# Attention into a cosine-gated FFN on one core: float64 weights turned into float32 in two engine passes instead of three, with the stored bytes shifted by two and a new hand order

## The chip, the cores and the metric

The kernel runs on one core of one Trainium2 chip. The metric is the device time of one execution in microseconds (us), the median of several runs. The kernel before takes 707.85 us (three runs, 706.53 to 709.95).

## What is computed

Eight batches, eight heads, 576 tokens, head size 64, 32 memory slots, then a feed-forward layer over all 4608 tokens:

```python
a = softmax(phi, axis=seq)                      # (b, h, s, m)
k_m = einsum('bhsm,bhsd->bhmd', a, k); v_m = einsum('bhsm,bhsd->bhmd', a, v)
attn = softmax(q @ k_m.T / sqrt(64)) @ v_m      # (b, h, s, d)
x = attn.transpose(0, 2, 1, 3).reshape(4608, 512)
h = x @ w_in                                    # w_in: 512 x 2048
out = (h * cos(h)) @ w_out                      # w_out: 2048 x 512
```

The inputs are float32, but `w_in` and `w_out` are float64: the drawn numbers are scaled without a cast. [...]

## The kernel before, in words

**Tiling.** The 4608 tokens are worked in 12 groups of 384, so that two batches of 576 make three groups. The hidden dimension of 2048 is cut into 16 slices f of 128. For each group and each f there is a first product (`gemm1`, tile `hp`), a chain on ScalarE (ACT) and VectorE (DVE) for h·cos(h) (tiles `gp` and `u`), and a second product (`gemm2`, tile `acc`) that adds up over f, four slices behind the first. `v_m` is folded into `w_in` beforehand (`fold_first` for group 0, tile `pvf`, kept as `vf`; `fold_psum` for the rest, tiles `pv` and `vw`), so that `gemm1` multiplies softmax weights (`aT`) by folded weights. Group 0 works in float32 on the converted weights as they are; from group 1 on every operand is split into a float16 high and low part, once the largest weight is known.

**Weights.** Each weight matrix comes in eight blocks, in0 to in7 and out0 to out7, 1024 KB of float64 each, 8 KB on each of 128 partitions. Blocks in2 and in3 are parked in the part of `wo` that later holds out6, out7 and out4, out5; the other fourteen take turns in three buffers, raw0 to raw2, and a load waits until its buffer's last block has been converted. Block in(j) is needed by fold_first(j), which serves gemm1 of slices 2j and 2j+1 of group 0; block out(j) by gemm2 of the same slices.

**Conversion before** (`conversion`, lines 156 to 185). Of each 8-byte word: *low* (L171 on ACT, L166 on DVE or POOL) writes the low 16 bits of the result from a byte of the lower word; *scale* (L175 on ACT, L176 on POOL) multiplies the upper word, read as float32, by 2^-112 in place, which moves the exponent; *sign* (L179, DVE) writes the upper 16 bits with the sign; *join* (L181, DVE) shifts the scaled word left by three and ORs it in. A *square* (L184, ACT) then sums the squares for the largest weight. That is four conversion instructions and a square for each of 16 blocks, each over 128x1024 elements.

**Order.** Group 0, the attention of batch 0 and the start of batch 1, the conversions and all their loads stand in one order written out by hand: the string `ORDER`, whose names are steps. Each engine runs its own steps in that order, and SyncE's (SP's) queue issues the loads in it. `warm*n` is n matmuls on zeros that keep TensorE (PE) busy and compute nothing; all 75 of them stand ahead of the first `gemm1`. From group 1 on a scheduler lays out the instructions.

The steps at the start, in the order of their dependence: load `phiT` and turn it into softmax weights (`max0`, `e0`, PE transposes `w0`, copies `k0`, L745); gather over tokens with the five loaded parts of k and v (`ga0_0` to `ga0_4`, L258, tile `psA`); normalise (`X0`, L780 and L782), transpose (`tpx0`, L787), spread into `km` (L270, L271) and `vm`; scores (`sc0`, L403) with the loaded `q`; on DVE transpose (`tu0`, L409), maximum (`mx0`, L413), subtract (`sh0`, L420), on ACT exp (`ex0`, L416), on DVE sum (`to0`, L424 to L426), normalise (`no0`, L430), transpose back (`ba0`, L434, into `aT`); and with the folded block in0 the first `gemm1` (`g1_0`, L561).

Of the kernel before, what the change touches and what calls it, by code (L numbers as in the profile page):

```python
# [23 lines left out]
P = 128  # L24
# [9 lines left out]
NW = DF // WS  # L34
GT = 384
# [8 lines left out]
LOW_ACT = set('in0 in2 in6 in7 out2 out3 out6 out7'.split())  # L44
LOW_POOL = set('in3 in4 out1 out4 out5'.split())
SCALE_ACT = set('in1 in2 in3 in4 in6 in7 out0 out5'.split())
COPY_ACT = set('vm1'.split())
# [27 lines left out]
def attention_then_ffn(ctx: ExitStack, tc: tile.TileContext, phi, phiT, kv, kv_first, qT, w_in, w_out, eye, out):  # L75
# [18 lines left out]
    w_in_sb = const.tile([P, NP, DF], F32, name="w_in_sb")  # L94
# [61 lines left out]
    def conversion(dst, raw, sq_to):  # L156

        high = raw[:, :, :, 1]  # L160
        flat = raw.rearrange("p c f t -> p c (f t)")
        halves = dst.bitcast(I16).rearrange("p c (f t) -> p c f t", t=2)
        low_top = flat.bitcast(U8).rearrange("p c (f t) -> p c f t", t=8)[:, :, :, 3]
        high_top = flat.bitcast(I8).rearrange("p c (f t) -> p c f t", t=8)[:, :, :, 7]
        def low_bits(engine):
            engine.tensor_scalar(out=halves[:, :, :, 0], in0=low_top, scalar1=2.0 ** -5, scalar2=-31.0 / 64.0,  # L166
                                 op0=ALU.mult, op1=ALU.add)

        spare = junk.rearrange("p (c f) -> p c f", c=dst.shape[1])
        return {  # L170
            "low_ACT": lambda: nc.scalar.activation(halves[:, :, :, 0], low_top, AF.Copy, scale=2.0 ** -5,  # L171
                                                    bias=-31.0 / 64.0),
            "low_DVE": lambda: low_bits(nc.vector),
            "low_POOL": lambda: low_bits(nc.gpsimd),
            "scale_ACT": lambda: nc.scalar.mul(high.bitcast(F32), high.bitcast(F32), 2.0 ** -112),  # L175
            "scale_POOL": lambda: nc.gpsimd.tensor_scalar(out=high.bitcast(F32), in0=high.bitcast(F32),  # L176
                                                          scalar1=2.0 ** -112, scalar2=1.0, op0=ALU.mult,
                                                          op1=ALU.mult),
            "sign": lambda: nc.vector.tensor_scalar(out=halves[:, :, :, 1], in0=high_top, scalar1=0.0,  # L179
                                                    scalar2=-32768.0, op0=ALU.is_lt, op1=ALU.mult),  # L180
            "join": lambda: nc.vector.scalar_tensor_tensor(out=dst.bitcast(I32), in0=high, scalar=3,  # L181
                                                           in1=dst.bitcast(I32), op0=ALU.logical_shift_left,
                                                           op1=ALU.bitwise_or),
            "square": lambda: nc.scalar.activation(spare, dst, AF.Square, accum_out=sq_to),  # L184
        }

    def convert(kind, j):
        if kind == "in":
            return conversion(w_in_sb[:, :, j * WS:(j + 1) * WS], loads.pop(("in", j)), sq[:, 0, j:j + 1])
        return conversion(wo[:, 2 * j + 1:2 * j + 3], loads.pop(("out", j)), sq[:, 1, j:j + 1])  # L190
# [32 lines left out]
    def w_in_split(q, c):  # L223
        if c == 0:
            st["parts"] = ld.tile([P, 2, NP, FS], F16, tag=f"raw{1 + q % 2}", name=f"w_in_parts_{q}")
        parts, s, src = st["parts"], st["s", "in"], w_in_sb[:, c, q * FS:(q + 1) * FS]
        nc.scalar.activation(parts[:, 0, c], src, AF.Copy, scale=s)
        nc.vector.scalar_tensor_tensor(out=parts[:, 1, c], in0=src, scalar=s, in1=parts[:, 0, c],
                                       op0=ALU.mult, op1=ALU.subtract)
        if c < NP - 1:  # L230
            return
        if q == 0:
            w2 = ld.tile([P, NP, 2, FS], F16, tag="raw0", name="w_in_2_0")
        else:
            w2 = w_in_sb[:, :, (q - 1) * FS:q * FS].bitcast(F16).rearrange("p c (o f) -> p c o f", o=2)
# [285 lines left out]
    def fold_first(j):  # L521
        pv = small_ps(f"pvf_{j}").rearrange("p (g x) -> p g x", g=2)
        for g in range(2):
            for i in range(2):
                c = 2 * g + i
                nc.tensor.matmul(pv[D * i:D * (i + 1), g], lhsT=st["vm", 0][:, c],  # L526
                                 rhs=w_in_sb[:, c, j * WS:(j + 1) * WS], start=True, stop=True)
# [331 lines left out]
    junk = wk.tile([P, 4 * WS], BF16, tag="aT", name="junk", bufs=3)  # L859
    for kind, j in blocks:  # L860
# [3 lines left out]
        def step(what, kind=kind, j=j, make=make):  # L864
            if not make:
                make.update(convert(kind, j))
            make[what]()
        low = "ACT" if name in LOW_ACT else "POOL" if name in LOW_POOL else "DVE"
        put(f"low_{name}", lambda step=step, low=low: step("low_" + low))
# [232 lines left out]
```

## Time and profile before

| What | Value |
|---|---|
| Median of three runs | 707.85 us (706.53 to 709.95) |
| The profiled execution's own time | 707.53 us |
| Its span (first to last instruction) | 705.4 us |
| PE busy | 695.0 us, 99% |
| DVE busy | 536.0 us, 76% |
| ACT busy | 515.6 us, 73% |
| POOL busy | 31.2 us, 4% |
| Moved by DMA | 66.17 MB |

Busy time is counted from the start of an instruction to its modelled end; PE's matmuls are pipelined, so a busy PE is not always a PE at its peak. The chain of waits is the work that ended last, followed back from the end: at each step to what released it. A row such as `L181 DVE ... x8 | 10.2, 1281 | 0.1` is a group of eight instructions of line 181, 10.2 us busy together, 1281 ns each, with 0.1 us of idle time of the engine before them. Where rows give a start, it is in us from the start of the span.

### The profile page before, as it was taken

The numbers are of one execution on the slowest core, as the hardware profiler recorded it, in microseconds if no ns is written. First come the engines' busy times: TensorE is split into PE (matmuls) and PEld (weight loads), VectorE is DVE, ScalarE is ACT, GpSimd is POOL, SyncE is SP. The second block draws the span as 40 slices with busy tenths as digits, with TensorE's granted clock in tenths as the row PEclk, the third lists the DMA queues.
The fourth block names the chain that finished last, engine by engine and source line by source line (L and its number), as shares of the span: only waits on it lengthen the run. The fifth ranks groups of instructions, "written<-read, shape, count | busy, mean of one in ns | idle before, by whom it ended". The sixth has DMA issues, their size and how long they took to land.

```text
span 705.4 us, 11869 instructions
## 1 busy us (share of the span) xinstructions
PE 695.0 (99%) x4607; PEld 355.9 (50%) x4607; DVE 536.0 (76%) x1130; ACT 515.6 (73%) x953; POOL 31.2 (4%) x43
## 2 busy tenths in 40 slices
PE   8999999999999999999999999999999999999997
PEld 3444455554444445655444445655444445565553
DVE  3899999999988876589667896579766986566552
ACT  3699897998985976869766885769757775665652
POOL 1122300000001000010000000000000000000000
PEclk9999999999999999999999999999999999999999
DMA  9998815128344200332105300152100100100101
GB/s 288 388 346 313 303 51 149 34 61 239 103 98 135 110 1 1 110 105 68 46 1 169 113 0 2 46 170 68 46 0 2 41 5 2 46 1 1 46 1 45
DMA packets 31480, 66.17 MB, mean 94 GB/s; under 512 B 2176, under 2 KB 11456, under 8 KB 31424
## 3 DMA queue, kind: packets, MB, share of 16 engines
q1 hardware_dynamic: 27104, 57.55, 25.4%
q10 hardware_dynamic: 4320, 7.87, 3.0%
q8 instruction: 36, 0.59, 0.4%
q14 instruction: 20, 0.16, 0.1%
HBM read 51.77 MB, written 9.44 MB: 87 GB/s over the span
## 4 chain that ended last, share of the span: by engine, by line
PE 82%; DVE 7%; ACT 7%; DMA 3%; issue 1%; SPq 0%; DVEq 0%; ACTq 0%
PE acc L621 40%; PE hp L570 22%; PE acc L616 6%; PE pv L500 4%; PE hp L561 3%; PE psA L258 3%; PE sc L403 2%; DMA phi<-in_phi 2%; DVE u L591 1%; PE warm L659 1%; ACT gp L586 1%; DMA raw_in<-in_w_in 1%; ACT u L596 1%; DVE u L600 1%; PE pv L494 1%; PE pvf L526 1%
## 5 line engine op out<-in xcount | busy, mean ns | idle before, releaser
L621 PE MATMUL acc<-wo,gp 128*128 128x512 f16 x1584 | 371.9, 379 | 0.0
L621 PEld LDWEIGHTS <-gp 128*128 128x128 f16 x1584 | 153.5, 98 | 159.3 <-issue 1.0
L570 PE MATMUL hp<-aT,vw 128*128 128x192 f16 (+1 forms) x1440 | 203.5, 284 | 1.6 <-DVE u L600 1.5
L570 PEld LDWEIGHTS <-vw 128*128 128x128 f16 x1440 | 124.9, 98 | 83.9 <-issue 29.1
L596 ACT ACTIVATE u<-u,quarter 128x384 f32<-128x384 f32 x176 | 106.7, 614 | 70.9 <-DVE u L591 70.4
L600 DVE SCALAR_TENSOR_TENSOR u<-hp,u 128x384 f32<-128x384 f32 x176 | 96.3, 553 | 60.8 <-ACT u L596 60.1
L591 DVE SCALAR_TENSOR_TENSOR u<-hp,cu,gp 128x192 f32<-128x192 f32 (+1 forms) x240 | 115.3, 503 | 23.7 <-ACT gp L586 22.1
L586 ACT ACTIVATE gp<-hp,cu 128x192 int32<-128x192 f32 (+1 forms) x240 | 110.9, 491 | 20.4 <-PE hp L570 15.2
L603 DVE TENSOR_TENSOR gp<-u,gp 128x384 f16<-128x384 f32 x176 | 96.1, 552 | 35.2 <-ACT gp L602 35.0
L602 ACT CAST gp<-u 128x384 f16<-128x384 f32 x176 | 88.0, 508 | 41.1 <-DVE u L600 40.4
L616 PE MATMUL acc<-wo,gp 128*128 128x512 f32 x96 | 44.4, 599 | 0.0
L509 DVE SCALAR_TENSOR_TENSOR vw<-pv,vw 128x512 f16<-128x512 f32 x48 | 33.0, 687 | 7.1 <-ACT vw L507 6.6
L507 ACT ACTIVATE vw<-pv 128x512 f16<-128x512 f32 x48 | 28.4, 591 | 8.7 <-PE pv L500 8.2
L637 ACT ACTIVATE ob<-acc,os 128x512 f32<-128x512 f32 x28 | 18.5, 684 | 14.8 <-PE acc L621 12.1
L616 PEld LDWEIGHTS acc<-wo,gp 128*128 128x128 f32 x96 | 17.5, 190 | 19.6 <-issue 16.3
L258 PE MATMUL psA<-kv,phi 128*32 128x129 f32 (+3 forms) x640 | 24.0, 277 | 1.1 <-ACT w_in_sb L171 0.6
L561 PE MATMUL hp<-aT,vf 128*128 128x384 f32 x64 | 23.9, 499 | 0.1
L596 ACT ACT_TABLE_LOAD x18 | 23.1, 1283 | 0.3
L258 PEld LDWEIGHTS psA<-kv,phi 128*32 128x32 f32 (+1 forms) x640 | 16.0, 109 | 13.8 <-issue 7.8
L659 PE MATMUL warm<-zeros 128*128 128x512 f16 x75 | 19.6, 402 | 1.8 <-DVE zeros L654 1.8
L403 PE MATMUL sc<-q,km 128*64 128x256 f32 (+3 forms) x192 | 20.0, 336 | 0.8 <-issue 0.8
L416 ACT ACT_TABLE_LOAD x14 | 18.0, 1283 | 0.2
(164 smaller groups left out, 550.8 us busy)
## 6 DMA issues: line engine op xcount, KB each, us to landing
kv<-in_kv SPq DMA_DIRECT2D x28, 516.0 KB, 6.4
raw_out<-in_w_out SPq DMA_DIRECT2D x8, 1024.0 KB, 7.2
q<-in_qT SPq DMA_DIRECT2D x7, 1152.0 KB, 5.6
out<-ob ACTq DMA_DIRECT2D x30, 256.0 KB, 2.1
raw_in<-in_w_in SPq DMA_DIRECT2D x6, 1024.0 KB, 9.8
phi<-in_phi SPq DMA_DIRECT2D x7, 512.0 KB, 6.1
w_in_sb<-w_in_parts SPq DMA_DIRECT2D x12, 256.0 KB, 5.6
phiT<-in_phiT SPq DMA_DIRECT2D x4, 576.0 KB, 7.8
```

The lines of the kernel that those rows point to most:

```text
L258: nc.tensor.matmul(psA[32 * j:32 * (j + 1), g * KV:g * KV + wide], lhsT=a[:n, c, h * M:(h + 1) * M], rhs=kvs[c][:n, h * wide:(h + 1) * wid ...
L403: nc.tensor.matmul(sc[D * p:D * (p + 1), g * n:(g + 1) * n], lhsT=km[:, 2 * g + p], rhs=qt[:, 2 * g + p, t0:t0 + n], start=True, stop=True)
L561: nc.tensor.matmul(hp[:, :GT], lhsT=st["vf", q][:, g, fo * P:(fo + 1) * P], rhs=st["aTf"][:, g], start=(g == 0), stop=(g == 1))
L570: nc.tensor.matmul(hp[:, c0:c0 + n], lhsT=vw[:, wi, g, fo * P:(fo + 1) * P], rhs=aT[:, ai, g, c1:c1 + n], start=(k == 0), stop=(k == 5))
L586: ins = nc.scalar.activation(ni[:, c0:c0 + n], hp[:, c0:c0 + n], AF.Copy, scale=turns, bias=0.25)
L591: nc.vector.scalar_tensor_tensor(out=u[:, c0:c0 + n], in0=hp[:, c0:c0 + n], scalar=turns, in1=ni[:, c0:c0 + n], op0=ALU.mult, op1=ALU.subt ...
L596: nc.scalar.activation(u, u, AF.Sin, scale=TWO_PI_BELOW, bias=quarter)
L600: nc.vector.scalar_tensor_tensor(out=u, in0=hp[:, :GT], scalar=2.0 ** -17, in1=u, op0=ALU.mult, op1=ALU.mult)
L602: nc.scalar.copy(gp[:, 0], u)
L603: nc.vector.tensor_tensor(out=gp[:, 1], in0=u, in1=gp[:, 0], op=ALU.subtract)
L616: nc.tensor.matmul(accs[grp][t], lhsT=gp[:, t * P:(t + 1) * P], rhs=wo[:, f + 1], start=(f == 0), stop=(f == NF - 1))
L621: nc.tensor.matmul(accs[grp][t], lhsT=gp[:, gi, t * P:(t + 1) * P], rhs=parts[:, wi], start=(f == 0 and gi == 0 and wi == 0), stop=(f == N ...
```

## The change

Four things change together.

**1. Two bytes on.** The weights are loaded as 16-bit words, 16 bytes of padding stand at the end of each raw buffer, and a block starts two bytes into its buffer (in2 and in3: two bytes ahead of their place in `wo`). So bytes 2 to 5 of each float64 are an aligned 32-bit word, which before they were not.

**2. Two passes.** *zero* clears the result block (16 memsets of 128x1024 float32, five on DVE, eleven on POOL; they don't depend on the load). *cast* reads the top 16 bits of each float64 as a bfloat16 and writes it as a float16 into the upper half of the result word: the change of format moves the exponent, with sign and top mantissa bits. *join* shifts the word of bytes 2 to 5 right by 13 and ORs it in. The square stays. Casts: four on ACT (in0, in1, in3, out2), three on DVE (in6, out1, out3), nine on POOL. So low, scale and sign go, cast and zero come, and the raw block is no longer written to. The copies `k0_1` and `vm0` move from DVE to ACT, and `vm1` the other way.

**3. Layout.** `w_in_sb` holds block after block, each contiguous, in place of one row of 2048 columns for each of four row groups; what reads 512 columns now reads two runs of 256.

**4. Order.** `ORDER` is new, and with it which engine gets which cast and zero. 56 warm matmuls stand ahead of the first `gemm1`, not 75.

```diff
-    w_in_sb = const.tile([P, NP, DF], F32, name="w_in_sb")
+    w_in_sb = const.tile([P, NW, NP, WS], F32, name="w_in_sb")
...
-        if j in (2, 3):
-            t = wo[:, 13:17] if j == 2 else wo[:, 9:13]
-            t = t.bitcast(I32).rearrange("p c (f t) -> p c f t", t=2)
+        if (kind, j) in PARKED:
+            t, s = wo.rearrange("p c f -> p (c f)").bitcast(I16), PARKED[kind, j] * 2 * DM - 1
         else:
-            t = ld.tile([P, NP, WS, 2], I32, tag=next_raw(), name=f"raw_in_{j}")
+            t, s = ld.tile([P, 4 * BW + 16], I16, tag=f"raw{next(raws) % 3}", name=f"raw_{kind}_{j}"), 1
...
+        nc.sync.dma_start(out=t[:, s:s + n].rearrange("p (c f) -> p c f", f=src.shape[2]), in_=src)
+        loads[kind, j] = t[:, s + 1:s + 1 + n]
...
+        words = dst.bitcast(I32).rearrange("p c f -> p (c f)")
+        upper = words.bitcast(F16).rearrange("p (f t) -> p f t", t=2)[:, :, 1]
+        top = raw.bitcast(BF16).rearrange("p (f t) -> p f t", t=4)[:, :, 2]
+        middle = raw.bitcast(I32).rearrange("p (f t) -> p f t", t=2)[:, :, 0]
...
-            "low_ACT": lambda: nc.scalar.activation(halves[:, :, :, 0], low_top, AF.Copy, scale=2.0 ** -5,
-                                                    bias=-31.0 / 64.0),
-            "scale_ACT": lambda: nc.scalar.mul(high.bitcast(F32), high.bitcast(F32), 2.0 ** -112),
-            "sign": lambda: nc.vector.tensor_scalar(out=halves[:, :, :, 1], in0=high_top, scalar1=0.0,
-                                                    scalar2=-32768.0, op0=ALU.is_lt, op1=ALU.mult),
-            "join": lambda: nc.vector.scalar_tensor_tensor(out=dst.bitcast(I32), in0=high, scalar=3,
-                                                           in1=dst.bitcast(I32), op0=ALU.logical_shift_left,
-                                                           op1=ALU.bitwise_or),
+            "cast_ACT": lambda: nc.scalar.copy(upper, top),
+            "cast_DVE": lambda: nc.vector.tensor_copy(out=upper, in_=top),
+            "cast_POOL": lambda: nc.gpsimd.tensor_copy(out=upper, in_=top),
+            "join": lambda: nc.vector.scalar_tensor_tensor(out=words, in0=middle, scalar=13, in1=words,
+                                                           op0=ALU.logical_shift_right, op1=ALU.bitwise_or),
...
-d_phiT0 max0 d_eye d_in0 e0_0 d_kv0_0 e0_1 d_kv0_1 warm*17 w0_0 d_kv0_2 scale_in0 w0_1 k0_1 d_kv0_3 k0_0 low_in0
+d_phiT0 d_eye zero_in2 max0 d_kv0_0 zero_out0 e0_0 e0_1 zero_in3 warm*17 w0_2 d_kv0_1 w0_1 zero_in5 zero_out1 k0_2
```

Where the new order differs is best seen at three places. First, the SP queue at the start of the program, before (`phiT_0` and `q_0` are the softmax input and the queries of batch 0, `kv_0_0` to `kv_0_4` the five parts of its k and v, `raw_in_0` is block in0, `wo_84` the parked block in2):

```order
L668 DMA phiT_0_96<-in_phiT 128x2x576
L671 DMA ident_76<-in_eye 128x128
L146 DMA raw_in_0_104<-in_w_in 128x4x512
L676 DMA kv_0_0_107<-in_kv_first 128x1024
L676 DMA kv_0_1_110<-in_kv_first 128x1024
L676 DMA kv_0_2_134<-in_kv_first 128x1024
L676 DMA kv_0_3_143<-in_kv_first 128x1024
L676 DMA kv_0_4_161<-in_kv_first 64x1024
L146 DMA raw_in_1_167<-in_w_in 128x4x512
L109 DMA q_0_229<-in_qT 128x4x384
L146 DMA wo_84<-in_w_in 128x4x512
L109 DMA q_0_229<-in_qT 128x4x192
```

And the same queue in the changed kernel:

```order
L651 DMA phiT_0_96<-in_phiT 128x2x576
L654 DMA ident_76<-in_eye 128x128
L659 DMA kv_0_0_105<-in_kv_first 128x1024
L659 DMA kv_0_1_131<-in_kv_first 128x1024
L659 DMA kv_0_2_143<-in_kv_first 128x1024
L659 DMA kv_0_3_145<-in_kv_first 128x1024
L659 DMA kv_0_4_148<-in_kv_first 64x1024
L107 DMA q_0_157<-in_qT 128x4x384
L148 DMA raw_in_0_159<-in_w_in 128x4x1024
L107 DMA q_0_157<-in_qT 128x4x192
L148 DMA raw_in_1_233<-in_w_in 128x4x1024
L148 DMA wo_84<-in_w_in 128x4x1024
```

Block in0 moves behind k, v and the first part of q, and in1 behind both parts of q; a dimension of 1024 for one of 512 is the same bytes counted as 16-bit words.

Second, DVE from the scores of batch 0 to the transposes back, before (`at_0` holds the softmax of batch 0, `w_in_sb` and `wo` the converted weights):

```order
L181 SCALAR_TENSOR_TENSOR w_in_sb_83<-raw_in_1_167,w_in_sb_83 128x4x256
L409 STREAM_TRANSPOSE at_0_248<-sc_0_0_265 128x512
L409 STREAM_TRANSPOSE at_0_248<-sc_0_256_273 128x256
L413 TENSOR_REDUCE rm_0_249<-at_0_248 128x24
L420 TENSOR_TENSOR at_0_248<-at_0_248,rm_0_249 128x768
L179 TENSOR_SCALAR w_in_sb_83<-wo_84 128x4x256
L424 TENSOR_REDUCE rs_0_250<-at_0_248 128x24
```

And in the changed kernel:

```order
L392 STREAM_TRANSPOSE at_0_229<-sc_0_0_238 128x512
L392 STREAM_TRANSPOSE at_0_229<-sc_0_256_250 128x256
L396 TENSOR_REDUCE rm_0_230<-at_0_229 128x24
L403 TENSOR_TENSOR at_0_229<-at_0_229,rm_0_230 128x768
L167 SCALAR_TENSOR_TENSOR w_in_sb_83<-raw_in_0_159,w_in_sb_83 128x1024
L407 TENSOR_REDUCE rs_0_231<-at_0_229 128x24
```

Before, the joins of in0 and in1 were done ahead of the scores and only the sign step of in2 stood between subtract and sum. Now the join of in0 stands there, and that of in1 follows the transposes back.

Third, ACT from the spreading of `km` to the second fold, before:

```order
L271 ACTIVATE km_0_225<-tpx_0_236 64x4x32
L175 ACTIVATE raw_in_1_167<-raw_in_1_167 128x1024
L175 ACTIVATE wo_84<-wo_84 128x1024
L416 ACTIVATE at_0_248<-at_0_248 128x768
L171 ACTIVATE w_in_sb_83<-wo_84 128x4x256
L534 COPY vf_0_299<-pvf_0_282 128x2x256
```

And in the changed kernel:

```order
L254 ACTIVATE km_0_182<-tpx_0_223 64x4x32
L261 COPY vm_0_183<-tpx_0_223 64x4x32
L262 COPY vm_0_183<-tpx_0_223 64x4x32
L164 CAST w_in_sb_83<-raw_in_0_159 128x1024
L399 ACTIVATE at_0_229<-at_0_229 128x768
L517 COPY vf_0_292<-pvf_0_284 128x2x256
L164 CAST w_in_sb_83<-raw_in_1_233 128x1024
```

The exp of batch 0 (L416, now L399) now stands behind the cast of block in0 on ACT. On PE the fold of block in1 moves from ahead of the first `gemm1` to behind it; 17 warm matmuls now stand between scores and the first fold, and three, not 14, between the transpose of X and the scores.

More of the change, by code (lines that the diff above doesn't have):

```diff
@@ L43 @@
 LAG = 4
[L44 to L47, printed above, removed]
+CAST_ACT = set('in0 in1 in3 out2'.split())
+CAST_POOL = set('in2 in4 in5 in7 out0 out4 out5 out6 out7'.split())
+ZERO_DVE = set('in2 in5 in6 out1 out2'.split())
+COPY_ACT = set('k0_1 vm0'.split())
 ORDER = """
-d_phiT0 max0 d_eye d_in0 e0_0 d_kv0_0 e0_1 d_kv0_1 warm*17 w0_0 d_kv0_2 scale_in0 w0_1 k0_1 d_kv0_3 k0_0 low_in0
@@ L187, in convert, with stretch, load_block @@
[L187 to L190, printed above, removed]
+    def stretch(kind, j):
+        return w_in_sb[:, j] if kind == "in" else wo[:, 2 * j + 1:2 * j + 3]
+    def load_block(kind, j):
+        if (kind, j) in PARKED:
+            t, s = wo.rearrange("p c f -> p (c f)").bitcast(I16), PARKED[kind, j] * 2 * DM - 1
+        else:
+            t, s = ld.tile([P, 4 * BW + 16], I16, tag=f"raw{next(raws) % 3}", name=f"raw_{kind}_{j}"), 1
+        n = 4 * BW
+        if kind == "in":
+            src = w_in[:, 4 * WS * j:4 * WS * (j + 1)].rearrange("(c p) f -> p c f", p=P)
+        else:
+            src = w_out[2 * P * j:2 * P * (j + 1)].rearrange("(c p) e -> p c e", p=P)
+        nc.sync.dma_start(out=t[:, s:s + n].rearrange("p (c f) -> p c f", f=src.shape[2]), in_=src)
+        loads[kind, j] = t[:, s + 1:s + 1 + n]
@@ L225, in w_in_split @@
             st["parts"] = ld.tile([P, 2, NP, FS], F16, tag=f"raw{1 + q % 2}", name=f"w_in_parts_{q}")
-        parts, s, src = st["parts"], st["s", "in"], w_in_sb[:, c, q * FS:(q + 1) * FS]
-        nc.scalar.activation(parts[:, 0, c], src, AF.Copy, scale=s)
-        nc.vector.scalar_tensor_tensor(out=parts[:, 1, c], in0=src, scalar=s, in1=parts[:, 0, c],
+        parts, s, src = st["parts"], st["s", "in"], w_in_sb[:, 2 * q:2 * q + 2, c]
+        high, low = (parts[:, k, c].rearrange("p (w f) -> p w f", w=2) for k in range(2))
+        nc.scalar.activation(high, src, AF.Copy, scale=s)
+        nc.vector.scalar_tensor_tensor(out=low, in0=src, scalar=s, in1=high,
                                        op0=ALU.mult, op1=ALU.subtract)
@@ L856, in attention_then_ffn @@
     attend_out(0, ((0, 1),))
[L859 removed]
+    junk = wk.tile([P, BW], BF16, tag="aT", name="junk", bufs=3)
     for kind, j in blocks:
@@ L865, in step @@
             if not make:
[L866 removed]
+                make.update(conversion(kind, j))
             make[what]()
[L868 to L872 removed]
+        zero = "DVE" if name in ZERO_DVE else "POOL"
+        put(f"zero_{name}",
+            lambda kind=kind, j=j, zero=zero: (nc.vector if zero == "DVE" else nc.gpsimd).memset(stretch(kind, j), 0.0))
+        cast = "ACT" if name in CAST_ACT else "POOL" if name in CAST_POOL else "DVE"
+        put(f"cast_{name}", lambda step=step, cast=cast: step("cast_" + cast))
         put(f"join_{name}", lambda step=step: step("join"))
```

85 lines of the change are left out of this document (29 added, 56 removed).

## The prediction

> **What bounds the kernel now.** I read the page's busy times first, then the table of windows, cut where the chain of waits changes its character, then the chain itself and the rows of the timeline around the first loads. The page's first rows, and the windows (columns: time, then busy us and instruction count of PE, its weight loads, DVE, ACT and POOL, granted clock, DMA share, GB/s):
>
> ```profile
> PE 695.0 (99%) x4607; PEld 355.9 (50%) x4607; DVE 536.0 (76%) x1130; ACT 515.6 (73%) x953; POOL 31.2 (4%) x43
> 0.00:31.10 31.10, 27.81 (x207) 12.65 (x207) 16.72 (x33) 14.52 (x22) 3.76 (x10) 1.00 0.97 329
> 31.10:98.90 67.80, 67.71 (x292) 32.00 (x293) 63.16 (x120) 60.73 (x100) 16.82 (x12) 1.00 0.81 282
> 135.00:200.00 65.00, 63.65 (x441) 33.16 (x440) 62.97 (x135) 58.84 (x111) 1.31 (x4) 1.00 0.39 109
> ```
>
> From 31.1 on PE hardly stops: 0.09 us of idle time to 98.9, where group 0 and all conversions lie, and 1.35 us from 135 to 200. DVE and ACT are 93% and 90% busy while the weights are converted, but PE never waits long for them, so quicker conversions by themselves save next to nothing there. What is left to win is ahead of 31.1: PE is 27.81 us "busy" there, mostly with warm matmuls. The chain (start, us, what) shows what that stage waits for:
>
> ```profile
> 1.73 7.39 DMA raw_in<-in_w_in
> ...
> 17.24 0.57 PE psA L258 x16
> ...
> 18.79 0.23 PE tpx L787 x2
> 19.02 3.02 PE warm L659 x14
> 22.04 1.04 PE sc L403 x8
> ...
> 23.10 1.06 DVE at L409 x2
> 24.18 0.96 DVE rm L413
> 25.17 0.97 DVE at L420
> 26.16 0.85 ACT at L416
> 27.03 0.96 DVE rs L424
> 28.57 1.83 DVE at L430
> ...
> 31.12 2.85 PE hp L561 x8
> 33.97 1.05 PE pvf L526 x8
> ```
>
> It goes from the gathers to the scores and the softmax of batch 0 on DVE; at 31.12 the first gemm1 (L561) starts, and PE is dense from then on. So my sum is: when does that matmul start in the changed kernel, and does PE stay dense behind it?
>
> **The change, part by part.** *Loads.* The first stage follows the DMA. These groups give the sizes:
>
> ```profile
> raw_in<-in_w_in SPq DMA_DIRECT2D x6, 1024.0 KB, 9.8
> phiT<-in_phiT SPq DMA_DIRECT2D x4, 576.0 KB, 7.8
> kv<-in_kv_first SPq DMA_DIRECT2D x4, 512.0 KB, 9.8
> q<-in_qT SPq DMA_DIRECT2D x1, 768.0 KB, 15.0
> q<-in_qT SPq DMA_DIRECT2D x1, 384.0 KB, 14.3
> kv<-in_kv_first SPq DMA_DIRECT2D x1, 256.0 KB, 11.8
> ident<-in_eye SPq DMA_DIRECT2D x1, 64.0 KB, 3.5
> ```
>
> and these rows of the timeline tell when a load was in, by the instruction that it released:
>
> ```profile
> 14.08 0.38 PEld L258 LDWEIGHTS psA<-kv,phi 128*32 128x32 f32 x16 [0.42 <-DMA kv<-in_kv_first]
> 15.84 0.38 PEld L258 LDWEIGHTS psA<-kv,phi 128*32 128x32 f32 x16 [0.42 <-DMA kv<-in_kv_first]
> 19.50 0.78 DVE L166 TENSOR_SCALAR w_in_sb<-raw_in 128x1024 int16<-128x1024 uint8 x1 [1.27 <-DMA raw_in<-in_w_in]
> 24.36 1.16 ACT L175 ACTIVATE wo<-wo 128x1024 f32<-128x1024 f32 x1 [3.50 <-DMA wo<-in_w_in]
> ```
>
> Summed in the order of issue, before: phiT, ident and in0 are 1664 KB, in by 9.1 (1.73 + 7.39); with three parts of k and v 3200 KB by 14.1; with four 3712 KB by 15.8; with the fifth and in1 4992 KB by 19.5; with q and in2 6784 KB by 24.4. The DMA share there is 0.97, so I take the same bytes to take the same time in the new order. All of k and v is then 576 + 64 + 2048 + 256 = 2944 KB: 9.1 + 5.0 x 1280/1536 = 13.3. The first part of q makes 3712 KB: 15.8. in0 makes 4736 KB: 15.8 + 3.7 x 1024/1280 = 18.8. in1, behind q's second part, 6144 KB: 22.6; in2 25.4; from there 2.8 us a block, out0 28.2, in3 31.0.
>
> *The chain to the first gemm1.* Before, from the last gather at 17.24 km is ready after 2.4 us:
>
> ```profile
> 19.39 0.27 ACT L271 ACTIVATE km<-tpx 64x128 f32<-64x128 f32 x1
> ```
>
> (19.39 + 0.27 - 17.24). Then 14 warm matmuls held PE until 22.04. Now km is ready at 13.3 + 2.4 = 15.7, three warm matmuls lie beside that, and the scores wait for q: 15.85. Transposes start 1.06 later as before (23.10 - 22.04), at 16.9; transposes, maximum and subtract take 3.0 as before (25.17 + 0.97 - 23.10), to 19.9. Here the new order puts the cast of in0 ahead of exp on ACT and the join of in0 ahead of the sum on DVE. The nearest rows for their prices:
>
> ```profile
> L171 ACT ACTIVATE w_in_sb<-raw_in 128x1024 int16<-128x1024 uint8 x3 | 4.1, 1366 | 0.1
> L184 ACT ACTIVATE junk<-w_in_sb 128x1024 bf16<-128x1024 f32 x8 | 8.4, 1046 | 1.6 <-DVE w_in_sb L181 1.6
> L181 DVE SCALAR_TENSOR_TENSOR w_in_sb<-wo,w_in_sb 128x1024 int32<-128x1024 int32 x2 | 2.4, 1212 | 0.5 <-DVE w_in_sb L179 0.5
> L179 DVE TENSOR_SCALAR w_in_sb<-raw_in 128x1024 int16<-128x1024 int8 x6 | 4.8, 800 | 1.6 <-POOL raw_in L176 1.5
> ```
>
> The cast on ACT lies between 1.05 (L184, contiguous) and 1.37 us (L171, the same strides); I take 1.37: 18.8 + 1.37 = 20.2. The join is unchanged in kind: 1.21, to 21.4; exp (0.85) runs beside it. The sum and its two small steps take 1.54 as before (28.57 - 27.03), to 23.0. The normalise took 1.83 us, while the subtract of the same shape took 0.97; I take 0.97, because POOL was at work only before:
>
> ```profile
> 28.29 1.36 POOL L166 TENSOR_SCALAR w_in_sb<-raw_in 128x1024 int16<-128x1024 uint8 x1 [16.71 <-ACT w_in_sb L171]
> 37.05 1.73 DVE L181 SCALAR_TENSOR_TENSOR wo<-raw_out,wo 128x1024 int32<-128x1024 int32 x1
> 30.43 1.16 DVE L434 STREAM_TRANSPOSE aT<-at 128x256 f32<-128x256 f32 x4
> ```
>
> That gives 23.95, and with the transposes back (1.16, all four needed in the new order) 25.1. Beside this PE folds in0 from 21.4 to 22.5, and the last scores and eight warm matmuls end about 25. First gemm1: 25.1, that is 6.0 us earlier. But the fold of in1, done before 31.12 until now, comes behind it: 1.05 us of PE's work (the chain's row at 33.97). Gain 5.0 us.
>
> *Dense behind it?* I followed the next ten steps with the same prices. Fold of in1: join in1 follows the transposes, 25.1 + 1.2 = 26.3, and PE wants it at 25.1 + 1.4 = 26.5. Fold of in2 is wanted at 30.4; its cast, on POOL, starts at 25.4, and with 1.4 us for it and the join behind it is ready at 29. gemm2 of slice 0 is wanted at 32.8; out0 is in at 28.2, cast by 29.6, joined behind two steps of group 0 at about 32.5. Fold of in3: wanted at 36.8, joined at about 35.5. So the cover is thin, 0.2 to 1.5 us, and then widens, as two slices with their two blocks take PE about 9 us (two of gemm1 at 1.43, two of gemm2 at 2.6, a fold) and the DMA 5.6. I count no loss, and 1 us if that cover goes.
>
> *The engines.* DVE loses 16 signs (0.8 us, L179) and three lows, gains three casts (taken as 0.8) and five memsets, these early in a stretch where it is busy for 16.7 of 31.1 us: 13 us less in all. ACT loses eight lows (1.37) and eight scales (about 1.18) and gains four casts: 15 us less.
>
> ```profile
> L175 ACT ACTIVATE raw_in<-raw_in 128x1024 f32<-128x1024 f32 x4 | 4.7, 1186 | 0.0
> L265 POOL MEMSET km<- 128x256 f32 x8 | 2.5, 310 | 58.4 <-PE sc L403 58.3
> ```
>
> Since PE does not wait for them from 31 to 99, the saving is worth at most the 1.35 us between 135 and 200, where PE runs out of the lag that it allows them. I take 0.5. POOL's memsets (310 ns for 256 elements, so some 1.2 us for 1024) need no load: five run before 7 us, six between casts. [...]
>
> The row at 28.29 bears on that: POOL worked to 29.65, and the normalise that DVE began at 28.57 came out 0.86 us longer; the join at 37.05 took 1.73, not 1.21. [...] By the rows alone: 13 POOL instructions cost DVE under 1 us each, and 15 behind the start hardly more. The sum stays.
>
> **Sum:** 5.0 + 0.5 = 5.5 us. Span 705.4 - 5.5 = 699.9; the execution took 707.53 us, 2.1 more than its span, and lies 0.3 from the median of 707.85. Predicted: 702.0 us.
>
> **The rivals.** *Slower: the shifted bytes slow the loads.* Every weight row now lands two bytes off an aligned place; no row here shows such a load. A block takes 2.8 us now (4.86 us for the 1792 KB from in1 to in2). With a factor f on it, in0 and so the first gemm1 come 2.8 (f - 1) later, and the stream of 16 blocks and some 7 MB of other loads, counted from 1664 KB at 9.1, ends at 9.1 + 19.3 + 44.8 f: at 73 for f = 1. PE wants block out7 converted at 102, five before this row of the chain, gemm2 of the last slice but one:
>
> ```profile
> 107.40 2.60 PE acc L616 x6
> ```
>
> At f = 2 it lands at 118, is converted near 120.5 and PE waits 18 us: 720 us. The whole gain is gone from f about 1.7. For it: the DMA share near 1 in the first 31 us leaves no slack. Against: bytes and rows are the same, and only the place differs. [...] Chance 0.10.
>
> *Little gain: the start is held.* in0 now hangs ahead of exp and sum, so each us by which it lands after 18.8 moves the first gemm1 one for one; or the thin cover breaks at several blocks, each worth about 1 us. With in0 at 21 and 1 us lost behind, the gain is 2.3: 705.2. For it: at 15.8 to 19.5 the stream moves slower (1280 KB in 3.7 us) than later. Against: the bytes ahead of in0 are fewer than ahead of in1 before. Chance 0.21.
>
> *More gain.* If the loads run at 2.8 us for 1024 KB from 9.1 on, k and v are in at 12.6, the scores start at 15.0 and in0 lands at 17.5; its cast lies beside the softmax and the first gemm1 comes at 23.9. With all of the 1.35: 5.0 + 1.2 + 1.35 = 7.5, and 700.0 us. Chance 0.09.
>
> **How the numbers follow.** The forecast (700.5 to 704) has 0.60, the held start 0.21, more gain 0.09, the slower loads 0.10. The range 698.8 to 706.5 leaves out the slower loads, the last part of the held start and the tail of the gain, about 2 in 10. Half a per cent, about what a measurement here can tell, is 3.5 us. Faster by more than that: 0.60 + 0.09 - 0.02 for forecasts at the edge = 0.67. Within: 0.22, the held start and that edge less 0.01. Slower: 0.11.
>
> **What would show it.** In the changed profile: the scores at 15.9, cast of in0 at 18.8 on ACT released by its DMA, join in0 to 21.4, the first gemm1 at 25, and from there a chain of PE rows without a gap. POOL busy for about 38 us (31.2, less 13 instructions of some 1.45, plus nine casts of 1.4 and eleven memsets of 1.2). I am wrong if in0 lands after 20, if a block takes over 4 us, if PE's idle time between the first gemm1 and the end of group 0 exceeds 1 us, or if gain comes from behind 99 us.

## The result, and the profile after

The changed kernel takes 700.78 us (median of four runs, 700.28 to 701.88) against 707.53 us (706.53 to 709.95) for the kernel before, run beside it. The ratio is 0.9902 with a 95% interval of 0.9874 to 0.993: faster by 1%, 6.75 us. 702.0 was forecast. Counted by instructions, a block's conversion goes from four to three: *zero*, *cast* and *join*, of which *zero* does not wait for the load.

The page's first row and the windows of the changed kernel; they are cut some 6 us earlier than those shown of before, since its first `gemm1` comes earlier by that:

```profile
PE 691.4 (99%) x4588; PEld 354.8 (51%) x4588; DVE 525.9 (75%) x1118; ACT 503.1 (72%) x942; POOL 36.9 (5%) x50
0.00:25.00 25.00, 22.79 (x180) 11.43 (x180) 15.37 (x34) 9.79 (x17) 5.21 (x11) 1.00 0.95 320
25.00:92.70 67.70, 67.67 (x297) 31.64 (x296) 54.06 (x105) 52.23 (x91) 20.72 (x18) 1.00 0.88 315
92.70:129.00 36.30, 36.28 (x223) 19.66 (x221) 35.27 (x79) 32.17 (x63) 0.31 (x1) 1.00 0.50 129
129.00:194.00 65.00, 64.43 (x443) 33.69 (x441) 63.10 (x135) 57.91 (x111) 1.41 (x3) 1.00 0.40 110
```

In the stretch of group 0 and the conversions (second window) DVE is busy for 54.06 us where it was 63.16, ACT for 52.23 where it was 60.73. PE is as dense as before: 0.05 us of idle time in the 104 us from 25 to 129. Between 129 and 194 its idle time is 0.57 us; in the same stretch before, 135 to 200, it was 1.35.

So the time has to come from the start, and the chain (start, us, what) shows it there:

```profile
13.78 0.57 PE psA L241 x16
...
15.61 0.65 PE warm L642 x3
...
16.36 1.10 PE sc L386 x8
17.49 1.06 DVE at L392 x2
...
19.55 0.82 DVE at L403
20.43 1.23 DVE w_in_sb L167
21.80 1.08 PE pvf L509 x8
...
25.39 1.53 PE hp L544 x4
26.92 1.01 PE pvf L509 x8
...
107.19 2.60 PE acc L599 x6
...
457.26 4.82 DMA phi<-in_phi
```

The first `gemm1` (L544) starts at 25.39, not at 31.12: 5.73 us earlier. The scores (L386) start at 16.36, not at 22.04: 5.68 us earlier. From the scores to the first `gemm1` it is 9.03 us now and was 9.08. **Net, all that was won at the start was won ahead of the scores.** The fold in the row behind (26.92, 1.01) was done ahead of the first `gemm1` before, which leaves 4.7 us. The rows of before that answer to the last two, in its chain:

```profile
112.12 2.60 PE acc L616 x6
...
462.32 6.08 DMA phi<-in_phi
```

At 107 us the lead is 4.93 us (112.12 - 107.19). It is 5.06 where the chain enters the load of `phi` of a later batch (462.32 - 457.26), and there the changed kernel gains once more: its load takes 4.82 us, that of before 6.08, which is 1.26 us. That makes 6.3, the difference of the two spans (705.4 and 699.1).

Why the scores can start earlier: first the row of SP's queue in the timeline of before, then of the changed kernel its group of that load (KB each, median us from issue to landing) and three rows of its timeline.

```profile
6.53 0.68 SPq L109 DMA_DIRECT2D q<-in_qT  x1
```

```profile
q<-in_qT SPq DMA_DIRECT2D x1, 768.0 KB, 11.2
```

```profile
4.22 0.58 SPq L107 DMA_DIRECT2D q<-in_qT  x1
...
15.99 0.27 ACT L254 ACTIVATE km<-tpx 64x128 f32<-64x128 f32 x1
...
18.98 1.35 ACT L164 CAST w_in_sb<-raw_in 128x1024 f16<-128x1024 bf16 x1 [2.29 <-DMA raw_in<-in_w_in]
```

Before, the first part of `q` was issued behind in0 and in1, at 6.53, and landed at 21.5 (with the 15.0 us that the prediction shows); the scores began at 22.04, when the 14 fillers ahead of them had ended. Now it lands at 15.4 (4.22 + 11.2), and the scores wait for something else, `km`, which ACT has ready at 16.26 (15.99 + 0.27), as the three fillers left there end too.

`km` itself is 3.4 us earlier than before, when it was ready at 19.66 (the row of L271 in the prediction, 19.39 + 0.27), because the last gather over k and v starts at 13.78 and not at 17.24. So an earlier `q` alone would not have made it: with `km` at 19.66 the scores could have come at most 2.4 us earlier. The last row is the cast of in0: it starts when its load lands, 18.98, and takes 1.35 us.

### The profile page after: what moved, and what is told of

Same layout as the page of the kernel before. It is cut to its first block, busy times and chain, and to the rows that moved or that the text cites. A ratio compares the mean times of both kernels' runs of the same rounds, so it can differ in the third digit from the quotient of the medians.

```text
span 699.1 us, 11806 instructions
## 1 busy us (share of the span) xinstructions
PE 691.4 (99%) x4588; PEld 354.8 (51%) x4588; DVE 525.9 (75%) x1118; ACT 503.1 (72%) x942; POOL 36.9 (5%) x50
## 4 chain that ended last, share of the span: by engine, by line
PE 81%; DVE 10%; ACT 4%; DMA 3%; issue 1%; SPq 0%; POOL 0%; DVEq 0%; ACTq 0%
PE acc L604 40%; PE hp L553 21%; PE acc L599 6%; PE pv L483 4%; PE hp L544 3%; PE psA L241 2%; DVE u L574 2%; PE sc L386 2%; DVE gp L586 1%; DMA phi<-in_phi 1%; DMA kv<-in_kv_first 1%; DVE u L583 1%; PE pvf L509 1%; PE pv L477 1%; ACT u L579 1%; ACT gp L585 1%
## 5 line engine op out<-in xcount | busy, mean ns | idle before, releaser
L544 PE MATMUL hp<-aT,vf 128*128 128x384 f32 x64 | 24.0, 499 | 0.0
L386 PE MATMUL sc<-q,km 128*64 128x256 f32 (+3 forms) x192 | 20.0, 336 | 0.1
L324 POOL PARTITION_ALL_REDUCE l<-l x6 | 3.0, 508 | 301.3 <-DVE l L270 301.3
```

Source lines behind the costliest of these rows:

```text
L386: nc.tensor.matmul(sc[D * p:D * (p + 1), g * n:(g + 1) * n], lhsT=km[:, 2 * g + p], rhs=qt[:, 2 * g + p, t0:t0 + n], start=True, stop=True)
L544: nc.tensor.matmul(hp[:, :GT], lhsT=st["vf", q][:, g, fo * P:(fo + 1) * P], rhs=st["aTf"][:, g], start=(g == 0), stop=(g == 1))
```

## The experiments

The theory after the result: the time is won because k, v and `q` are all in earlier, so that the scores can start, and is kept only because the lighter conversion leaves DVE and ACT room behind an earlier start. Rivals: the order alone makes it; the two passes alone make it; the aligned or shifted place of the bytes matters; the start doesn't matter, since the conversions pace group 0. In this table the ratio is to the kernel before, with its 95% interval (it goes by the means, so it need not be the ratio of the medians), and PE's idle time is 104 us less what its rows show busy from 25 to 129 us (a wait for a later first `gemm1` included).

| Run | us, median | ratio | first `gemm1` | PE idle, 25 to 129 |
|---|---|---|---|---|
| the changed kernel | 700.78 | 0.9902 (0.9874 to 0.993) | 25.39 | 0.05 |
| e1_in0_first | 701.66 | 0.9946 (0.991 to 0.9981) | 25.92 | 0.03 |
| e2_old_passes | 711.81 | 1.0048 (1.0028 to 1.0068) | 26.59 | 6.05 |
| e3_two_passes | 708.74 | 1.001 (0.9989 to 1.0031) | 33.07 | 2.15 |
| e5_work_back | 714.31 | 1.0085 (1.0055 to 1.0114) | 25.25 | 11.11 |
| e5a_vector_pass | 707.27 | 0.999 (0.9969 to 1.0011) | 25.07 | 6.94 |
| e5b_scalar_pass | 706.53 | 0.9985 (0.9969 to 1.0) | 25.14 | 3.71 |
| e4_aligned | 700.34 | 0.9902 (0.988 to 0.9924) | 25.08 | 0.05 |
| e7_late_start | 706.17 | 0.9989 (0.9972 to 1.0006) | 28.84 | 0.71 |
| e6_no_filler | 701.94 | 0.991 (0.9882 to 0.9937) | 25.39 | 0.44 |
| f1_shift_18 (one run) | 709.21 | | 30.31 | 1.89 |
| f2_shift_24 (one run) | 712.16 | | 32.62 | 2.00 |
| b1_before_again (one run) | 706.6 | | 30.50 | 0.25 |

**in0 loaded first again.** In the order of the changed kernel:

```diff
-d_phiT0 d_eye zero_in2 max0 d_kv0_0 ... d_q0_0 d_in0 k0_0 ...
+d_phiT0 d_eye zero_in2 max0 d_in0 d_kv0_0 ... d_q0_0 k0_0 ...
```

> The changed kernel with one load moved: block in0 is issued ahead of k and v again, as before the change; all else is as changed. If the gain comes from the order of the loads: k and v are complete at 17 us and the first part of q at 18.9 us in place of 15.4, so the scores start near 19.7 us, not 16.4, the first gemm1 near 28.7, not 25.4, and the time is 3.3 us above the changed kernel's 700.8: 704.1 us. If the gain comes from less work on VectorE and ScalarE: within 1 us of 700.8.

It measured 701.66 us as a median, 0.9 above the changed kernel and not the 3.3 expected. But its seven executions lie apart: four took 701.1 to 701.66, three 706.36 to 708.46. By the means it is 2.9 above (703.86 against 700.93). So the time leaves open what the place of in0 is worth. The profile is of an execution of 701.52; its chain:

```profile
16.89 1.52 PE sc L386 x16
...
25.92 1.53 PE hp L544 x4
```

The scores come 0.53 us later, not the 2.7 us of a whole block. Its groups of loads show why:

```profile
q<-in_qT SPq DMA_DIRECT2D x1, 768.0 KB, 11.4
```

Issued at 4.78, `q` lands at 16.2, with 4736 KB moved; in the changed kernel the same bytes, in another order, were in only when in0 landed, at 18.96. So "the same bytes take the same time" holds only to some 2.8 us here. But `q` still stood ahead of in1 in this run. In this execution the place of in0 is worth half a us; what made the three long ones long is not shown.

**The old passes with the new loads and first steps.** The kernel before, its loads and first steps put in the order of the changed kernel up to the first `gemm1`; the rest of the order stays (it was not searched anew for this mix):

```diff
-d_phiT0 max0 d_eye d_in0 e0_0 d_kv0_0 ... d_in1 ... d_q0_0 ... sc0_0 ...
+d_phiT0 d_eye max0 d_kv0_0 ... d_q0_0 d_in0 ... d_q0_1 d_in1 warm*3 sc0_0 ... scale_in0 low_in0 ... join_in0 ...
```

> The kernel before, with its four-instruction conversion and its layout, but the loads and the first steps in the changed kernel's order. If the order of the start makes the gain: the sign step of in0 lies on the chain (0.8 us), the first gemm1 comes near 26.2 us, PE stays dense, and the time is 4.1 us under the kernel before: 703.4 us. If the shorter conversion is needed for PE to stay dense after an earlier start: PE idles over 2 us between the first gemm1 and the end of group 0, and the time is 705 us or more.

711.81 us: slower than before. Its window and its chain behind the first `gemm1`:

```profile
25.00:92.70 67.70, 61.69 (x279) 28.28 (x277) 58.72 (x113) 56.45 (x90) 17.39 (x15) 0.97 0.85 303
```

```profile
15.72 1.10 PE sc L402 x8
...
26.59 2.82 PE hp L560 x8
29.41 1.04 PE pvf L525 x8
...
31.05 1.27 ACT w_in_sb L170
...
36.64 2.00 DVE wo L180
...
38.69 4.54 PE acc L615 x6
```

The start is nearly as early as in the changed kernel: scores at 15.72, first `gemm1` at 26.59. But then the chain leaves PE for ACT's *low* of a block (31.05) and DVE's join (36.64, 2.00 us long), and PE stands idle for 6 us by 92.7. The new order of the start alone, with the rest of the steps as they stood, makes the early start and cannot keep it.

**Two passes in the old order.** The changed kernel's code with the order of before (*scale* replaced by *zero*, *sign* by *cast*, *low* dropped):

```diff
-d_phiT0 d_eye zero_in2 max0 d_kv0_0 zero_out0 ...
+d_phiT0 max0 d_eye d_in0 e0_0 d_kv0_0 e0_1 d_kv0_1 warm*17 w0_0 d_kv0_2 zero_in0 ...
```

> The changed kernel's two-pass conversion, layout and shifted blocks in the order of the kernel before: zero stands where scale stood, cast where sign stood, low is gone. If the order of the start makes the gain: the scores still wait for 14 warm matmuls and for q until 22 us, the first gemm1 comes at 30 to 31 us, and the time is 706.5 to 707.5 us. If the shorter conversion makes the gain: 703 us or less.

708.74 us, ratio 1.001: no difference that can be measured, and if anything the dearer side. In this order the conversion alone saves nothing net. Its chain has two new rows ahead of the first `gemm1`:

```profile
22.09 1.04 PE sc L386 x8
...
24.04 0.91 DVE w_in_sb L850
...
29.13 1.10 DVE rs L408
...
30.58 1.77 DVE at L413
...
33.07 2.85 PE hp L544 x8
```

A *zero* on DVE (24.04) stands between two transposes of the softmax, and a small step that takes 0.19 us in the changed kernel takes 1.10 (L408), the normalise 1.77 (L413), each while POOL works on a block (a memset from 29.22 to 30.18, a cast from 30.25 to 31.59, a memset from 31.48). So the first `gemm1` comes 1.95 us later than before (33.07 for 31.12). Behind it that lag is made up: the chain enters the load of `phi` at 462.28, before at 462.32. Part of it lies between 129 and 194 us:

```profile
129.00:194.00 65.00, 64.68 (x459) 34.95 (x458) 63.33 (x136) 59.00 (x113) 1.29 (x4) 1.00 0.34 101
```

PE idles for 0.32 us here, and for 1.35 in the same window of the kernel before. What two passes bring in an old order that keeps *zero* out of the softmax was not run, so a gain of a us or two by the conversion alone is not ruled out.

**The saved work put back.** The changed kernel with a pass of the old sign's form on DVE ahead of each join but in0's, and a second square on ACT for each block but in0; neither result is used. Then each alone:

```diff
+            if (kind, j) != ("in", 0) and what == "join":
+                make["again"]()
             make[what]()
+            if (kind, j) != ("in", 0) and what == "square":
+                make[what]()
```

> The changed kernel with the saved work given back as work without use: for every block but in0 one more VectorE pass of the old sign step's form ahead of the join, and a second square on ScalarE, some 11 us and 18 us more. If PE bounds all that follows the first gemm1: VectorE is 95% busy while the weights are converted and the time is at most 1.5 us above 700.8. If the freed engines make the gain: 4 us or more of it are lost, 705 us.

> The changed kernel plus one more pass of VectorE (the form of the old sign's pass, its result unused) ahead of each join but the first; ScalarE has its new work only. Both passes put back cost 13.5 us. Theory A (either engine is enough to break the thin cover, VectorE has 80% between 25 and 93 us): 704 to 708, TensorE idle over 2 us between 25 and 93. Theory B (the loss was ScalarE's alone, whose second squares were 19% of the chain in the first 60 us): within 1.5 of 700.8.

> The changed kernel plus a second square on ScalarE for each block but the first (unused); VectorE has its new work only. Theory A (either engine is enough): 704 to 710, TensorE idle over 2 us between 25 and 93. Theory B (the loss was ScalarE's alone): 710 or more. If both this and the VectorE pass stay within 1.5 of 700.8, only the two together break the cover.

Both passes: 714.31 us, 13.5 above the changed kernel. DVE's alone: 707.27, 6.5 above. ACT's alone: 706.53, 5.75 above. Theory A stands: either engine is enough, and each takes back nearly the whole gain. The windows from 25 to 92.7, DVE's pass first, then ACT's:

```profile
25.00:92.70 67.70, 62.97 (x276) 29.73 (x276) 62.12 (x102) 44.85 (x80) 19.06 (x18) 0.97 0.86 300
```

```profile
25.00:92.70 67.70, 65.07 (x288) 30.06 (x288) 49.90 (x96) 60.47 (x108) 20.27 (x18) 1.00 0.91 315
```

With DVE back at 62.12 us of 67.7, or ACT at 60.47, close to what they had before (63.16 and 60.73), PE idles for 4.7 and 2.6 us there, where before it idled for 0.09. About as much work, harmless with the late start, breaks the cover with the early one.

Two limits of these runs. The profile of DVE's pass is of an execution of 710.58 us, the longest of ten, so its idle time is on the high side. And there the unused pass takes 0.7 us at its quickest (39.54) but 2.4 ahead of the join of in1 (24.92); why is not shown. Two waits of PE, 3.0 us for that join and 2.2 for the join of out0, make most of its 6.94 us of idle time. So the run prices a pass in this place, not busy time as such. In the run with ACT's squares, which stand behind the joins, the squares are 23% of the chain from 25 to 129 us.

**Blocks at the exact place.** The shift of two bytes taken away:

```diff
-            t, s = wo.rearrange("p c f -> p (c f)").bitcast(I16), PARKED[kind, j] * 2 * DM - 1
+            t, s = wo.rearrange("p c f -> p (c f)").bitcast(I16), PARKED[kind, j] * 2 * DM
-            t, s = ld.tile([P, 4 * BW + 16], I16, tag=f"raw{next(raws) % 3}", name=f"raw_{kind}_{j}"), 1
+            t, s = ld.tile([P, 4 * BW + 16], I16, tag=f"raw{next(raws) % 3}", name=f"raw_{kind}_{j}"), 2
-        loads[kind, j] = t[:, s + 1:s + 1 + n]
+        loads[kind, j] = t[:, s:s + n]
-        top = raw.bitcast(BF16).rearrange("p (f t) -> p f t", t=4)[:, :, 2]
+        top = raw.bitcast(BF16).rearrange("p (f t) -> p f t", t=4)[:, :, 3]
```

> The changed kernel with every weight block at the exact place (no two bytes on): the top 16 bits are then read as the upper half of their own word, and the bits below them stay what they were, so the weights are right to about four mantissa bits only; the number, order and sizes of all operations are the same. Theory (the shift costs the loads nothing, 2.6 to 2.7 us a block with it and without): 700.8, within 1 us, loads of 2.6 to 2.7 us a block. Rival (the shift slows the writes of the loads a little, and the first loads bind): blocks of 2.4 us or less, first first-layer matmul before 25.0, 699.5 or less.

700.34 us, 0.44 below and well inside what the runs can tell. Its window:

```profile
25.00:92.70 67.70, 67.67 (x297) 31.82 (x297) 53.96 (x104) 52.56 (x92) 20.43 (x18) 1.00 0.88 313
```

The DMA share is 0.88 and the rate 313 GB/s; the changed kernel has 0.88 and 315. The shift costs nothing that shows here.

**A later start.** Fourteen more filler matmuls ahead of the first scores, then eighteen and twenty-four:

```diff
-... d_q0_1 d_in1 warm*3 sc0_0 ...
+... d_q0_1 d_in1 warm*17 sc0_0 ...
```

> The changed kernel with 14 more filler matmuls (0.216 us each in its trace: 3.0 us) ahead of the first scores, so that everything from the scores on starts 3 us later, while loads and conversions go on. Theory (the earlier start is on the path one for one, and from it on TensorE has no idle time to give back): 703.5 to 704.0, first first-layer matmul at 28.4. Rival (the conversions and loads pace the first group, so that a later start is made up by 100 us): within 1 of 700.8, because the gain at 100 us is back at about 5 us.

> The changed kernel with 18 more filler matmuls (3.9 us) ahead of the first scores, so that the kv and phi loads near 460 us are issued at about 458.2, where the kernel before issued them (458.19). If the time of issue decides how long the load of phi takes: 5.5 us or more, and the second kv load holds SyncE for 1.3 us. If the old order decides: 4.8 to 5.3 us, and the third kv load is the one that holds it. The whole: 706.5 to 707.5.

> The changed kernel with 24 more filler matmuls (5.2 us) ahead of the first scores: kv loads issued at about 459.5, where the run with the second squares put back issued them (459.22) and its load of phi was quick. If the time of issue decides: 4.8 to 5.3 us. If any later start of this kernel makes the load slow: 5.5 or more. The whole: 707 to 708.5.

706.17, 709.21 and 712.16 us (the last two single executions): 5.4, 8.4 and 11.4 above the changed kernel for 3.0, 3.9 and 5.2 us of filler. So nothing of a later start is made up; my numbers were too low. The chain of the first of them:

```profile
15.56 3.67 PE warm L642 x17
19.23 1.04 PE sc L386 x8
...
23.24 1.22 DVE w_in_sb L167
...
25.91 1.60 DVE at L413
...
28.84 1.54 PE hp L544 x4
```

The filler comes to 3.67 us in place of 0.65; the normalise (25.91) now falls beside POOL's cast of in2 (25.37, 1.38 us) and takes 1.60, where it took 0.96 in the changed kernel. The first `gemm1` is 3.45 late, and the lag of the spans is 5.0. Of the rest, 0.7 comes between there and the load of `phi` (entered at 461.43), where no cause was traced, and 0.75 at that load (5.57 for 4.82). In the run with eighteen, DVE and POOL at that place:

```profile
25.61 1.21 DVE L408 TENSOR_SCALAR rs<-rs 128x24 f32<-128x24 f32 x1
...
27.19 1.79 DVE L413 TENSOR_TENSOR at<-at,rs 128x768 f32<-128x768 f32 x1
```

```profile
24.32 1.61 POOL L166 CAST w_in_sb<-wo 128x1024 f16<-128x1024 bf16 x1 [18.58 <-DMA wo<-in_w_in]
25.83 0.95 POOL L850 MEMSET w_in_sb<- 128x1024 f32 x1
26.88 1.34 POOL L166 CAST wo<-raw_out 128x1024 f16<-128x1024 bf16 x1
```

A step of 24 elements a partition takes 1.21 us and ends when POOL's memset does (26.78). Then the normalise ends 0.8 us late beside the cast. In the changed kernel POOL's casts begin at 25.71, just when this chain has passed.

**Without the fillers.** The 17 and 8 `warm` matmuls between the first scores and the first `gemm1` dropped:

```diff
-... ex0_0 join_in0 warm*17 ff0 ... join_in1 warm*8 g1_0 ...
+... ex0_0 join_in0 ff0 ... join_in1 g1_0 ...
```

> The changed kernel without the 25 filler matmuls (17 and 8, 5.4 us of TensorE) between the first scores and the first first-layer matmul, where TensorE then waits for the softmax and the first join. Theory (they only fill a wait that VectorE's chain and the join set): 700.8 within 1 us, first first-layer matmul at 25.4, granted clock 1.0 behind it. Rival (the wait without them lowers TensorE's clock when the folds and the first layer begin, as the older passes' kernel with its idle stretches showed 0.97 between 25 and 93): granted clock under 0.98 between 25 and 93 us, 702 to 705.

701.94 us; the timed runs cannot tell it from the changed kernel, its profile can, and shows half of each theory. Its windows and PE's rows:

```profile
0.00:25.00 25.00, 18.79 (x155) 9.79 (x155) 15.37 (x34) 9.13 (x17) 5.21 (x11) 0.91 0.94 324
25.00:92.70 67.70, 67.28 (x293) 31.57 (x292) 53.39 (x104) 51.70 (x90) 20.33 (x18) 0.98 0.90 314
```

```profile
21.79 1.98 PE L509 MATMUL pvf<-w_in_sb,vm 128*64 128x256 f32 x8 [3.91 <-DVE w_in_sb L167]
...
25.39 2.54 PE L544 MATMUL hp<-aT,vf 128*128 128x384 f32 x4 [0.34 <-DVE aT L417]
28.02 1.08 PE L509 MATMUL pvf<-w_in_sb,vm 128*64 128x256 f32 x8
```

The first `gemm1` starts at 25.39 as ever, but the granted clock has dropped (0.91, then 0.98 as a mean), and its four matmuls take 2.54 us in place of 1.53. The rest follows about 1.1 us late. The fold ahead of that `gemm1`, behind 3.91 us in which PE stood idle, took 1.98 us for 1.08 (the chain's row at 21.80 in the changed kernel), and the next fold (28.02) 1.08 again. So in this run the wait without fillers went with a lower granted clock, and cost 1.1 us; what sets the clock is not shown.

**The load of `phi` at 460 us.** The kernel before, run once more:

> The kernel before, looked at once more, for the 1.26 us that the changed kernel gains at 462 to 468 us, where a load of phi stands in the chain (6.08 us before, 4.82 after, 4.8 to 5.3 in six other profiles, 6.96 and 5.57 in the two passes in the old order and in the late start). If the slow load belongs to this kernel: 5.5 to 7 us again, and the second of the kv loads ahead of it holds SyncE for 1.3 us. If it is chance: any value, 4.8 to 5.3 the likeliest.

```profile
461.92 5.57 DMA phi<-in_phi
```

5.57 us again. Over all profiles this load took 4.8 to 5.2 us in the changed kernel and in all seven variants that keep its loads or steps and start at the same time (4.82, 4.94, 4.98, 5.06, 5.22, 5.11, 4.86 and 4.94), and 5.57 to 6.96 us in the six others (before 6.08 and 5.57, the old order 6.96, the three late starts 5.57, 6.47 and 6.38). It does not follow the conversion (the old passes with the new start were quick, the two passes in the old order slow), nor the old order (the late starts were slow too). It does not follow the time of issue: in the run with twenty-four the chain enters the load at 466.94 and it was slow (6.38), in the run with DVE's pass at 466.63 and it was quick (5.11). In these fourteen profiles it goes with the start: quick where the first `gemm1` comes by 26.6, slow where it comes from 28.8 on. That the early start makes it quick is not shown. What decides it stays open; it is 1.26 us of the 6.3.

## Why the prediction was right, and where its steps were not

**"Quicker conversions by themselves save next to nothing there"** held on balance: two passes in the old order measured 1.001, though with a later start of their own in it. The prediction priced the lighter engines as a term, worth "at most the 1.35 us between 135 and 200", and took 0.5. There PE's idle time fell by 0.78 us (0.57 for 1.35), and by 1.03 with the two passes in the old order; but the lead from 107 to 457 us grew by 0.13 only. DVE's saving, put at 13 us, measured 10.1 (536.0 to 525.9; the five memsets, named there, were not subtracted), ACT's, put at 15, 12.5. The larger part was missed: without the lighter engines there would have been no 5.0. The sentence "I count no loss, and 1 us if that cover goes" is the step that was mis-sized. The cover did hold, at 0.05 us of idle time. But its price was 5.75 to 6.5 us for one pass on one engine, not 1: in the DVE run two single waits cost 3.0 and 2.2 us, where the rival of the held start had put a broken block at about 1.

**Loads.** The landings were right for this order: `q` at 15.4 (forecast 15.8), in0 at 18.96 (18.8). The reason given, that "the same bytes take the same time", fell with the run that loads in0 first: 4736 KB were in by 16.2 there and by 18.96 here. So that the landings came out is luck, as far as these runs show.

**The chain.** Scores "wait for q: 15.85" came at 16.36, and not `q` but `km` was last (ACT's row at 15.99, ending 16.26, together with the fillers). The join of in0 ended at 21.66 (21.4), the normalise took 0.96 (0.97), and the first `gemm1` came at 25.39 (25.1). Gain there, less the fold: 4.7, with 4.93 by 107 us, for 5.0.

**POOL beside DVE.** The prediction took it from two rows of before that work of POOL costs DVE under 1 us at a time, and hardly more behind the start than it had before. The two did meet: in the changed kernel the cast of in2 on POOL starts at 25.71 beside the join of in1.

```profile
25.71 1.85 POOL L166 CAST w_in_sb<-wo 128x1024 f16<-128x1024 bf16 x1 [19.97 <-DMA wo<-in_w_in]
28.37 2.00 POOL L166 CAST wo<-raw_out 128x1024 f16<-128x1024 bf16 x1
34.10 1.88 DVE L167 SCALAR_TENSOR_TENSOR w_in_sb<-wo,w_in_sb 128x1024 int32<-128x1024 int32 x1
```

Instructions came out longer where the two met (casts of 1.85 and 2.00 us for 1.35, a join of 1.88 for 1.22), but POOL lost mostly, off the path: PE idled for 0.05 us from 25 to 129. The 24-element step that took 1.21 us beside a memset of POOL, above, is one more such meeting. That POOL's work is the cause was the author's reading of such rows; no run here takes that work away and leaves the rest as it stands.

**The rivals.** The slower loads did not happen (700.78 and 700.34 us at the two places of the bytes). The held start did not either: in0 landed before 20. More gain did not come in the way of its rival: the scores started at 16.36, not 15.0. "Wrong if gain comes from behind 99 us": 1.26 us did, at the load of `phi`, and another 0.13 between 107 and 457 us. Without the load of `phi` the sum of 5.5 us would have met 5.04. No step of the prediction has that load, so the measured gain lies above the forecast by luck.

## What to carry to other kernels

When the bound engine is dense behind a start, move the start; but ask in the same breath what the engines behind it must then deliver, since work that was covered by the late start is not covered by the early one. Price a thin cover by breaking it, with one unused pass a block on one engine: here it was worth six times the estimate. A change of order and a change of work that gain nothing apart, in the orders tried here, can gain together, so test each alone before giving either the credit.

## What the runs showed that was not expected

- The same first eight loads in the same order, 3968 KB, were in by 17.0 us before (the fifth part of k and v: issued at 5.22, 11.8 us to landing) and by 14.2 in the run that loads in0 first in the changed kernel (issued at 4.19, 10.0 us). In each profile the rate falls for a while, to 150 to 270 GB/s at a DMA share still near full (90% or more in each slice of the views): from 12.4 to 16.3 us before, from 12.4 to 14.0 in that run, from 10.1 to 13.2 in the changed kernel. Why stays open.
- A later start cost 1.8, 2.2 and 2.2 us for each us of filler (5.4 for 3.0, 8.4 for 3.9, 11.4 for 5.2), in three parts. Up to the first `gemm1`, 0.4 us were added to the filler in the first run, where the normalise of batch 0 takes 1.60 us beside POOL's cast, and 2.0 in the last, where the step of 24 elements takes 1.22 us and the normalise 1.77. The slower load of `phi` added 0.75 and 1.56. Between the two another 0.7 and 2.45 were lost, without a cause found.
- A load whose every row lands two bytes off an aligned place took no longer than one at an aligned place: 315 and 313 GB/s between 25 and 92.7 us, 700.78 and 700.34 us.
